# A tile's first matmul of the feed-forward stage in two pieces of 512 columns instead of eight of 128

## The chip, the cores and the metric

One core of a Trainium2 chip runs the whole kernel. The metric is the device time of one launch in microseconds (us); lower is better. The times before are the median, the lowest and the highest of 3 runs.

## What is computed

Four sets of 12608 tokens (128 features each) go through a set attention with 32 learned points, and then through a feed-forward block whose activation is a softmax times its own input, followed by a normalization.

```python
def mab(q, kv):
    s = scale * (q @ kv.transpose(0, 2, 1))
    s = s - s.max(-1, keepdims=True)
    a = np.exp(s)
    a /= a.sum(-1, keepdims=True) + 1e-09
    return a @ kv
h = mab(I, x)          # the 32 points look at a set's 12608 tokens
x = mab(x, h)          # each token looks at the set's 32 points
...
h = x @ w_in           # 128 -> 1024
e = np.exp(h - max(h))
solu = h * (e / sum(e))
ln = (solu - mean) / sqrt(var + 1e-06) * g_ln
out = ln @ w_out       # 1024 -> 128
```

Since the second attention only mixes 32 rows, the kernel multiplies these rows with `w_in` once for each set (`hs`, 32 x 1024, kept four times, once for each group of 32 partitions). A token's `x @ w_in` is then its 32 attention weights times `hs`: a matmul that contracts over 32 rows alone.

## The kernel before

**Tiles.** Tokens are worked in tiles of 128, 396 tiles in all (99 in each of 4 sets), four tiles to a group. For one tile, in this order: the first matmul (TensorE, line 1233) gives 128 x 1024 in PSUM (`h`, four such buffers of two banks each); VectorE (line 1275) multiplies by the softmax's divisor and takes the minimum; ScalarE (1286) takes the exponential and its sum; GpSimd (1290) multiplies the two; ScalarE (1301) squares for the variance; VectorE (1317) transposes in blocks of 32 x 32. When a group's four tiles are there, TensorE makes the second matmul (line 1473, called the products here) with `w_out`, again contracting over 32 rows at a time, 32 steps of four matmuls.

**Row groups.** TensorE's array is used as four strips of 32 rows (row groups 0 to 3), taken as two pairs: 0 and 1, 2 and 3. A tile's first matmul uses one pair, by the parity of the tile's place: row group `r` makes columns 0 to 511 in the first bank of `h`, `r + 1` columns 512 to 1023 in the second. Both of its pieces are 32 x 128 weights (`aT`, the tile's attention weights) against `hs`. The products of one half of a group use the same pair throughout, and two such streams (one for each pair) are under way most of the time.

**Order.** A planner written into the kernel fixes each engine's order of instructions before the launch. On TensorE it works in beats. A beat of products is one step of one or both streams (two or four matmuls of 129 columns). The function `beats` lays the first matmul's pieces between product steps of the other pair, called its companions here:

```python
for i in range(count):
    if also:
        also(i)
    went = 0
    for w in pairs:
        p = going(w, plan.now + i * BEAT)
        if p:
            p["emit"](2 * w, p["j"])
            p["emit"](2 * w + 1, p["j"])
            p["j"] += 1
```

Here `count` is 4, `pairs` is the other pair alone, and `also` is the function that the change touches. What the planner takes a beat to cost does not depend on `also`'s pieces. In the program, 350 of the 396 first matmuls have companions in all four beats, 21 in one to three, and 25 have none.

An f32 matmul appears in the trace as two instructions (called passes here), each with a weight load of its own in front (the weight load has its own row, PEld). So a first matmul is 16 passes before, eight on each of its two row groups.

Of the kernel before, what the change touches and what calls it, by code (L numbers as in the profile page):

```python
# [19 lines left out]
P = 128  # L20
# [121 lines left out]
class Planner:  # L142
# [8 lines left out]
    def spawn(self, gen, prio):  # L151
        self._step([gen, prio, 0], None)
# [8 lines left out]
    def give(self, lock, buf, *after):  # L161
        lock.free.append((buf, after))
        while lock.free and lock.waiting:
            lock.waiting.sort(key=lambda w: (w[2], w[1]))
            task = lock.waiting.pop(0)[0]
            self.blocked -= 1
            self._step(task, lock.free.pop(0))
# [96 lines left out]
def set_attention_then_solu_kernel(ctx: ExitStack, tc: tile.TileContext, x, inducing, w_in, w_out, g_ln, out):  # L264
# [30 lines left out]
    def buf(shape, name, dtype=F32, where=None):  # L295
        return (where or const).tile(shape, dtype, name=name)
# [66 lines left out]
    quarter = buf([P, 4], "quarter")  # L363
# [772 lines left out]
    def going(w, at):  # L1136

        for p in stream[w]:
            if p["j"] < JB:
                return p if p["ready"] <= at + EAGER else None  # L1140
        return None

    def load(w):
        return going(w, plan.now) is not None

    def beats(count, pairs=(0, 1), also=None):

        flow["took"] = 0
# [10 lines that stand above are left out]
                    went += 1  # L1159
            if not (went or also):  # L1160
                return i
            full = went + bool(also) > 1
            flow["took"] += BEAT + (TURN_ON if full and flow["half"] else 0)
            flow["half"] = not full
        return count

    def closing(d):

        for w in range(2):
            while stream[w] and stream[w][0]["j"] == JB:  # L1170
                flow["left"] -= 1
                stream[w].pop(0)["close"](d)
# [25 lines left out]
    def main():  # L1198
        t = 0
        for b in range(NB):  # L1200
            for j in order[b]:
                left = list(range(ff_groups[j][1]))
                spawn(open_group(b, j), t)
                while left:
                    for item in starts.get(t, ()):
                        spawn(*item)
                    near = left[:WINDOW_TILES]
                    rel = []
                    for s in near:
                        d = yield aT_ready[(b, ff_groups[j][0] + s)]  # L1210
                        rel += d
                    d = yield hw_ready[b]
                    rel += d
                    _, turn = yield TURN
                    hp, hrel = yield H.at(t + H_LAST)
                    op = Op("PE", 4 * BEAT, None, rel, hrel, prio=t - 50)
                    chosen = []

                    def mm1():
                        def slot(s):  # L1220
                            return part_of[b, ff_groups[j][0] + s][1]

                        s = min(near, key=lambda s: (load(slot(s) % 2), s))
                        chosen.append(s)
                        ka, i = part_of[b, ff_groups[j][0] + s]
                        aT, hs = aT_of[(b, ka)]["aT"][0], hT[b][1]
                        r = i % 2 * 2

                        def quarter(c):
                            for k in range(2):  # L1230
                                rows = slice((r + k) * M, (r + k + 1) * M)
                                cols = slice(k * 512 + c * P, k * 512 + (c + 1) * P)
                                nc.tensor.matmul(hp[:, cols], lhsT=aT[rows, i // 2, :], rhs=hs[rows, cols], start=True, stop=True)  # L1233

                        beats(4, (1 - i % 2,), quarter)
                        op.cost = flow["took"]

                    op.fn = mm1
                    d = yield op
                    closing(d)  # L1240
                    s = chosen[0]
                    left.remove(s)
                    if not left and j == order[b][-1]:
                        give(HW, hT[b], d)
                    spawn(soft(t, b, j, s, hp, d), t)
                    t += 1

    def open_group(b, j):
        G = grp[(b, j)]
        vt, rel = yield VT  # L1250
        plan.set(G["vt"], *rel)
        G["vtb"] = vt
        if fin_of[b, j][1] == 0:
            spawn(open_finish(b, fin_of[b, j][0]), 0)
        st, rel = yield ST
        G.update(st)
        G["stb"] = st
        plan.set(G["st"], *rel)
# [421 lines left out]
```

## Time and profile before

| | |
|---|---|
| time, median of 3 runs (lowest to highest) | 1202.43 us (1199.68 to 1202.57) |
| time of the profiled execution | 1208.28 us |
| its span, first to last instruction | 1206.5 us |
| mean granted TensorE clock | 0.987 of full speed |
| busy: TensorE, weight loads, VectorE, ScalarE, GpSimd | 97%, 90%, 90%, 92%, 88% |

Busy shares are of the span. A matmul's duration in the trace holds the time to run through the array, so that one instruction's duration is longer than the step to the next on the same row group, and several row groups at work count as one busy engine: 97% is not four full row groups.

### The profile page before, as it was taken

What the parts mean: (1) busy time and instruction counts of PE and PEld (TensorE: products, weight loads), DVE (VectorE), ACT (ScalarE), POOL (GpSimd) and SP (SyncE); (2) the same over time, 40 slices, a digit from 0 to 9 for tenths busy, and PEclk for the clock granted to TensorE, in tenths of its full rate; (3) what the DMA queues carried; (4) which work ended last, traced back from release to release, by engine and by line L of the source; (5) the groups of instructions that cost most, each with busy time, mean ns of one, the idle gap of its engine ahead of it and who ended that gap; (6) DMA issues with size and microseconds to landing.
All of it is one profiled execution on the core that took longest, in us unless ns stands there. A gap on an engine that the chain in (4) does not pass through costs nothing.

```text
span 1206.5 us, 77701 instructions
## 1 busy us (share of the span) xinstructions
PE 1166.9 (97%) x35388; PEld 1087.0 (90%) x35388; DVE 1079.9 (90%) x1639; ACT 1105.3 (92%) x2191; POOL 1063.6 (88%) x612
## 2 busy tenths in 40 slices
PE   8999999999999999999999999999999999999997
PEld 6789989999899899999898989899989999999996
DVE  6779889899899899989899898989999999899991
ACT  4689898999999999989998999999999999999995
POOL 2288789899899989898898998989999999999995
PEclk9959999999999999999999999999999999999999
DMA  9531433332132433332413343233312122220203
GB/s 342 211 125 53 131 83 101 108 105 56 49 97 69 141 110 117 102 89 61 117 40 101 92 139 118 86 106 89 99 40 81 42 46 57 75 64 6 48 6 86
DMA packets 166922, 111.24 MB, mean 92 GB/s; under 512 B 78112, under 2 KB 131776, under 8 KB 166464
## 3 DMA queue, kind: packets, MB, share of 16 engines
q1 hardware_dynamic: 166592, 106.27, 30.4%
q8 instruction: 277, 4.54, 1.6%
q14 instruction: 53, 0.43, 0.1%
HBM read 53.51 MB, written 52.17 MB: 88 GB/s over the span
## 4 chain that ended last, share of the span: by engine, by line
PE 47%; POOL 13%; ACT 10%; issue 4%; DVE 3%; DMA 1%; SPq 0%; ACTq 0%; POOLq 0%; DVEq 0%
PE h L1473 33%; POOL eu L1290 10%; PE h L1233 9%; ACT sq L1301 4%; ACT eu L1286 3%; POOL spare L1290 2%; PE h L655 1%; POOL spare L1547 1%; ACT spare L1501 1%; DVE hn L1275 1%; DVE vt L1317 1%; PE h L733 1%; PE h L850 1%; DVE spare L1275 1%; PE h L991 1%
## 5 line engine op out<-in xcount | busy, mean ns | idle before, releaser
L1473 PE MATMUL h<-wc,vt 32*128 32x129 f32 (+1 forms) x25344 | 996.2, 273 | 18.6 <-issue 10.7
L1473 PEld LDWEIGHTS h<-wc,vt 32*128 32x128 f32 (+1 forms) x25344 | 962.7, 185 | 46.2 <-issue 26.3
L1290 POOL TENSOR_TENSOR eu<-hn,eu 128x1024 f32<-128x1024 f32 x198 | 467.0, 2379 | 44.8 <-ACT eu L1286 43.7
L1233 PE MATMUL h<-hs,aT 32*128 32x128 f32 x6336 | 437.4, 277 | 5.7 <-issue 2.3
L1233 PEld LDWEIGHTS h<-hs,aT 32*128 32x128 f32 x6336 | 392.7, 189 | 22.5 <-issue 5.8
L1317 DVE STREAM_TRANSPOSE vt<-eu 128x1024 f32<-128x1024 f32 x327 | 397.2, 1228 | 8.6 <-POOL eu L1290 8.1
L1301 ACT ACTIVATE sq<-eu 128x1024 bf16<-128x1024 f32 x330 | 346.4, 1050 | 10.6 <-POOL eu L1290 5.5
L1290 POOL TENSOR_TENSOR eu<-spare,eu 128x1024 f32<-128x1024 f32 x132 | 311.8, 2378 | 14.7 <-ACT eu L1286 14.7
L1275 DVE TENSOR_SCALAR_CACHE_REDUCE hn<-h,rn 128x1024 f32<-128x1024 f32 x198 | 249.4, 1263 | 31.8 <-PE h L1233 23.2
L1275 DVE TENSOR_SCALAR_CACHE_REDUCE spare<-h,rn 128x1024 f32<-128x1024 f32 x198 | 248.9, 1263 | 30.2 <-PE h L1233 15.5
L1286 ACT ACTIVATE eu<-hn,nm 128x1024 f32<-128x1024 f32 x198 | 225.4, 1139 | 3.4 <-DVE hn L1275 3.1
L1290 POOL TENSOR_TENSOR spare<-spare 128x1024 f32<-128x1024 f32 x66 | 156.9, 2378 | 13.8 <-ACT spare L1286 13.8
L1286 ACT ACTIVATE eu<-spare,nm 128x1024 f32<-128x1024 f32 x132 | 150.4, 1140 | 2.4 <-DVE vt L1317 1.3
L1317 DVE STREAM_TRANSPOSE vt<-spare 128x1024 f32<-128x1024 f32 x65 | 80.0, 1231 | 1.5 <-POOL spare L1290 1.5
L1547 POOL TENSOR_TENSOR spare<-spare,fin 128x512 f32<-128x512 f32 x79 | 79.8, 1042 | 1.6
L1301 ACT ACTIVATE sq<-spare 128x1024 bf16<-128x1024 f32 x66 | 69.3, 1050 | 7.0 <-POOL spare L1290 5.4
L1286 ACT ACTIVATE spare<-spare,nm 128x1024 f32<-128x1024 f32 x66 | 75.2, 1140 | 0.5 <-DVE spare L1275 0.5
L1301 ACT ACTIVATION_READ_ACCUMULATOR sq<-eu 128x1 f32 x330 | 62.6, 190 | 0.0
L1501 ACT COPY spare<-h 128x774 f32<-128x774 f32 (+3 forms) x66 | 42.6, 648 | 13.6 <-PE h L1473 11.0
L655 PE MATMUL h<-ident,xn 32*128 32x32 f32 x1188 | 54.0, 227 | 0.7 <-issue 0.7
L655 PEld LDWEIGHTS h<-ident,xn 32*128 32x128 f32 x1188 | 51.1, 141 | 1.0 <-issue 1.0
L666 ACT COPY xT<-h 128x1024 f32<-128x1024 f32 (+2 forms) x42 | 38.0, 905 | 10.4 <-PE h L655 9.3
(189 smaller groups left out, 849.4 us busy)
## 6 DMA issues: line engine op xcount, KB each, us to landing
out_dram<-spare SPq DMA_DIRECT2D x95, 256.0 KB, 3.6
xT<-xd SPq DMA_DIRECT2D x93, 256.0 KB, 3.8
xn<-in_x_dram SPq DMA_DIRECT2D x73, 256.0 KB, 4.0
xd<-xT SPq DMA_DIRECT2D x72, 256.0 KB, 2.7
dl<-dd SPq DMA_DIRECT2D x392, 1.0 KB, 2.8
xd<-vt SPq DMA_DIRECT2D x7, 768.0 KB, 10.1
spare<-in_x_dram SPq DMA_DIRECT2D x5, 768.0 KB, 11.0
dd<-qe SPq DMA_DIRECT2D x95, 4.0 KB, 2.0
```

What stands on the lines that cost most here:

```text
L655: nc.tensor.transpose(out=tr[:, k * 512 + s * M : k * 512 + (s + 1) * M], in_=xn[r, s, :], identity=ident[r, r])
L666: lambda: nc.scalar.copy(xT.rearrange("c s (q t) -> c q s t", q=4)[:, 2 * w : 2 * w + 2, :n, :], tr.rearrange("c (k x) -> c k x", k=2)[:, ...
L733: nc.tensor.matmul(sc[g * M : (g + 1) * M, : nn * M], lhsT=indT, rhs=xT[:, :nn, g * M : (g + 1) * M], start=True, stop=True)
L1233: nc.tensor.matmul(hp[:, cols], lhsT=aT[rows, i // 2, :], rhs=hs[rows, cols], start=True, stop=True)
L1275: lambda: nc.vector.tensor_scalar(out=hn, in0=hp, scalar1=rn, scalar2=None, op0=ALU.mult, op1=ALU.min, accum_out=nm),
L1286: "ACT", 1133, lambda: nc.scalar.activation(e, hn, AF.Exp, bias=nm, scale=-1.0, accum_out=G["qe"][:, s, 1:2]), d, rel, srel,
L1290: d = yield Op("POOL", 2330, lambda: nc.gpsimd.tensor_tensor(out=e, in0=hn, in1=e, op=ALU.mult), de, prio=t + PR_MU)
L1301: "ACT", 1040, lambda: nc.scalar.activation(sq, e, AF.Square, scale=1.0 / 32.0, accum_out=G["qe"][:, s, 0:1]), d,
L1317: lambda: nc.vector.transpose(out=G["vtb"][:, : n * FF].rearrange("p (j s t) -> p j s t", j=M, s=n)[:, :, s, :], in_=e.rearrange("p (a f) ...
L1473: nc.tensor.matmul(op[:rows, a - 2 * w, :], lhsT=vt[q, k, :], rhs=wc[q, k, :], start=(k == 0), stop=(k == JB - 1))
L1501: return lambda: eng(to, at)
L1547: return lambda: eng.tensor_tensor(out=raw, in0=raw, in1=y[:, i0 : i0 + 4].unsqueeze(2).to_broadcast([rows, 4, C]), op=ALU.mult)
```

## The change

Each of the two row groups makes its 512 columns in one matmul. Both are issued in the first beat, ahead of the first companion; the companions of the other three beats follow with nothing in between.

```diff
-                        def quarter(c):
-                            for k in range(2):
+                        def whole(c):
+                            for k in range(2 if c == 0 else 0):
                                 rows = slice((r + k) * M, (r + k + 1) * M)
-                                cols = slice(k * 512 + c * P, k * 512 + (c + 1) * P)
+                                cols = slice(k * 512, (k + 1) * 512)
                                 nc.tensor.matmul(hp[:, cols], lhsT=aT[rows, i // 2, :], rhs=hs[rows, cols], start=True, stop=True)
 
-                        beats(4, (1 - i % 2,), quarter)
+                        beats(4, (1 - i % 2,), whole)
```

The order of the instructions changes on TensorE alone; on the other engines and in the DMA queues it is the same. On TensorE at a first matmul with companions, early in the first set, rows with - stand in the program before, with + in the changed one (`h_732` is the tile's buffer, `h_733` and `h_731` those of the two product streams, x2 means two matmuls):

```order
 L1473 MATMUL h_731<-wc,vt 128x129 x2
-L1233 MATMUL h_732<-hs,aT_94 128x128 x2
-L1473 MATMUL h_733<-wc,vt 128x129 x2
-L1233 MATMUL h_732<-hs,aT_94 128x128 x2
-L1473 MATMUL h_733<-wc,vt 128x129 x2
-L1233 MATMUL h_732<-hs,aT_94 128x128 x2
-L1473 MATMUL h_733<-wc,vt 128x129 x2
-L1233 MATMUL h_732<-hs,aT_94 128x128 x2
-L1473 MATMUL h_733<-wc,vt 128x129 x4
+L1233 MATMUL h_732<-hs,aT_94 128x512 x2
+L1473 MATMUL h_733<-wc,vt 128x129 x10
 L1473 MATMUL h_731<-wc,vt 128x129 x2
```

The four companion steps (eight matmuls; the last two of the ten belong to the next beat) now stand behind the whole first matmul. On TensorE at the start of the feed-forward stage there are no products yet, and first matmuls follow one another:

```order
 L991 MATMUL h_730<-vt,h_0_117 32x256 x4
-L1233 MATMUL h_732<-hs,aT_94 128x128 x8
-L1233 MATMUL h_733<-hs,aT_94 128x128 x8
-L1233 MATMUL h_730<-hs,aT_94 128x128 x8
+L1233 MATMUL h_732<-hs,aT_94 128x512 x2
+L1233 MATMUL h_733<-hs,aT_94 128x512 x2
+L1233 MATMUL h_730<-hs,aT_94 128x512 x2
```

There, eight matmuls become two at the same place.

## Rows read from the trace of the kernel before

**Rows 1.** The page's head: span, busy time of each engine.

```profile
span 1206.5 us, 77701 instructions
PE 1166.9 (97%) x35388; PEld 1087.0 (90%) x35388; DVE 1079.9 (90%) x1639; ACT 1105.3 (92%) x2191; POOL 1063.6 (88%) x612
```

**Rows 2.** Busy time by stretch; the first line names the columns.

```profile
core 0: us, PE busy (x) PEld busy (x) DVE busy (x) ACT busy (x) POOL busy (x), PEclk, DMA share, GB/s
...
120.00:1030.00 910.00, 889.37 (x28286) 833.40 (x28282) 840.58 (x1244) 861.66 (x1696) 834.64 (x474) 1.00 0.32 89
1030.00:1175.00 145.00, 142.58 (x4698) 139.52 (x4696) 137.26 (x181) 140.07 (x275) 144.84 (x79) 1.00 0.17 39
```

**Rows 3.** The page's chain that ended last: shares of the span.

```profile
PE 47%; POOL 13%; ACT 10%; issue 4%; DVE 3%; DMA 1%; SPq 0%; ACTq 0%; POOLq 0%; DVEq 0%
PE h L1473 33%; POOL eu L1290 10%; PE h L1233 9%; ACT sq L1301 4%; ACT eu L1286 3%; POOL spare L1290 2%; PE h L655 1%; POOL spare L1547 1%; ACT spare L1501 1%; DVE hn L1275 1%; DVE vt L1317 1%; PE h L733 1%; PE h L850 1%; DVE spare L1275 1%; PE h L991 1%
```

**Rows 4.** Groups of instructions, forms apart: count, busy us, mean ns, idle before.

```profile
L1473 PE MATMUL h<-wc,vt 32*128 32x129 f32 x24320 | 959.1, 274 | 17.6 <-issue 10.7 <-ACT spare L1501 2.8 <-DVE spare L1501 1.2
L1233 PE MATMUL h<-hs,aT 32*128 32x128 f32 x6336 | 437.4, 277 | 5.7 <-issue 2.3 <-DVE spare L1275 1.4 <-ACT aT L1072 0.7
...
L1233 PEld LDWEIGHTS h<-hs,aT 32*128 32x128 f32 x6336 | 392.7, 189 | 22.5 <-issue 5.8 <-DVE hn L1275 4.1 <-DVE spare L1275 2.8
```

**Rows 5.** TensorE in order of time, a first matmul with companions: start, length.

```profile
602.84 0.38 PE L1233 MATMUL h<-hs,aT 32*128 32x128 f32 x2
602.93 0.39 PE L1473 MATMUL h<-wc,vt 32*128 32x129 f32 x4
603.05 0.28 PE L1233 MATMUL h<-hs,aT 32*128 32x128 f32 x2
603.15 0.27 PE L1473 MATMUL h<-wc,vt 32*128 32x129 f32 x2
...
603.71 0.28 PE L1473 MATMUL h<-wc,vt 32*128 32x129 f32 x2
603.73 0.28 PE L1233 MATMUL h<-hs,aT 32*128 32x128 f32 x2
```

**Rows 6.** TensorE, matmuls of 512 columns one after another (line 933).

```profile
588.04 1.02 PE L933 MATMUL h<-w_in_sb,h 128*128 128x512 f32 x2
588.47 1.02 PE L933 MATMUL h<-w_in_sb,h 128*128 128x512 f32 x2
```

**Rows 7.** The chain between 488 and 500 us: start, share of chain.

```profile
490.39 0.10 PE h L1233
490.51 0.10 PE h L1233
...
491.07 0.11 PE h L1233 x2
```

**Rows 8.** The longest waits on TensorE's first matmul: us, times, longest.

```profile
DVE hn L1275 <- PE h L1233: 23.2, 28, 2.8
DVE spare L1275 <- PE h L1233: 15.5, 25, 1.4
```

**Rows 9.** TensorE, line 544, four matmuls of 512 columns on four row groups.

```profile
45.93 0.71 PE L544 MATMUL bank_e<-hn,fold 32*128 32x512 f32 x4
45.93 1.14 PE L544 MATMUL bank_e<-hn,fold 32*128 32x512 f32 x8
L544 PE MATMUL bank_e<-hn,fold x8: 587/640/692, 45.9 to 46.5; 32*128 32x512 f32 x8
```

**Rows 10.** VectorE at the first tiles: start, length, idle time before.

```profile
55.50 1.28 DVE L1275 TENSOR_SCALAR_CACHE_REDUCE hn<-h,rn 128x1024 f32<-128x1024 f32 x1 [0.17 <-PE h L1233]
56.71 0.08 DVE L1275 DVE_READ_ACCUMULATOR hn<-h,rn 128x1 f32 x1
56.71 1.28 DVE L1275 TENSOR_SCALAR_CACHE_REDUCE hn<-h,rn 128x1024 f32<-128x1024 f32 x1
```

## The prediction

> **What bounds the kernel now.** I read the head of the page first, then the busy time by stretch, then the chain that ended last, then the single instructions. The head [rows 1] shows no engine that stands out: all five rows lie between 88% and 97%. The stretches [rows 2] say more. From 120 to 1030 us, three quarters of the span, ScalarE is busy for 861.66 of 910 us (95%), GpSimd for 834.64 (92%), VectorE for 840.58 (92%). From 1030 to 1175 us GpSimd is busy for 144.84 of 145 us: there nothing that TensorE does can help, as long as it isn't late. TensorE's own 889.37 of 910 can't be read as a share of its capacity, because two row groups at work look as busy as four. So I go to the chain [rows 3]: 47% of the span runs through TensorE, 33% through the products of line 1473 and 9% through the first matmul of line 1233; GpSimd has 13%, ScalarE 10%. TensorE's order sets the end for about half of the time, in the long middle stretch, and three other engines are a few per cent behind it. That is what limits any gain on TensorE: it is paid on the chain's share, and soon the next engine is the latest.
>
> What a first matmul costs on its two row groups is read from two places. With companions [rows 5] its passes start at 602.84, then 603.05, and from there to 603.73 in six steps: 0.68 / 6 = 0.113 us for 128 columns (the first step is 0.21 us long, since the first weight load has nothing to hide behind). On the chain [rows 7] it is the same: 490.39 to 491.07 in six steps. The companions keep the same step beside it (602.93, 603.15, ..., 603.71). So eight passes take 8 x 0.113 = 0.90 us.
>
> **What the change removes.** Of 6336 passes with as many weight loads [rows 4] a quarter stays, 1584 of each. The trace has no first matmul of 512 columns, but the nearest row shows what a pass of that length takes on a row group when its weights are there in time: on line 933 the starts are 588.04 and 588.47, a step of 0.43 us [rows 6]. That is 128 rows deep, not 32; the one place with 32 rows and 512 columns [rows 9] agrees: four matmuls on four row groups, eight passes, in 1.14 us, where the first passes last 0.692 and the second 0.587. The second four end at 47.07, so their starts are 47.07 - 0.59 = 46.48, 0.55 after the first; 0.692 - 0.587 = 0.105 of it is the weight load in front, which leaves 0.44, with up to 0.02 of the four's own spread in it. So two passes take 0.86 us in place of 0.90: **0.04 us less on the pair for each tile**. The 392.7 us of weight loads of line 1233 [rows 4] mostly disappear as busy time, but they are worth no more than this: they lay beside the passes, and that a pass of 128 columns steps at 0.113 where a quarter of 0.43 would be 0.108 is all that they can have cost.
>
> **What it adds.** Nothing. No instruction, wait or DMA is added, and the order on the other four engines is the same.
>
> **What it moves.** With companions (350 of 396 first matmuls in all four beats) the second to fourth companion stood behind a piece of the first matmul; now all stand behind the whole of it. Whether they start as early depends on whether TensorE lets an instruction for idle row groups pass one that waits for its own. Each first matmul puts two passes on each row group: the second must wait 0.43 us for the first, and everything behind it in the program belongs to the other pair. Line 544 [rows 9] decides this as far as a row here can. In the program its four matmuls follow one another, each with its two passes; in the first 0.1 us four passes have started, all at 45.93, and all eight are over after 1.14 us. Were the second matmul held until the first one's second pass had started, the four would need five steps of 0.43 us, 2.15 us and the run through the array. So TensorE does let later row groups pass. What that place doesn't show is a stream of short passes, sixteen of them, running past a long one that waits. Bounds for the companions: from below, nothing (they keep their step of 0.113); from above, they are held for one pass, 0.43 us. I take nothing, since the row is much nearer to it.
>
> The Trainium skill has a rule that speaks against this: "TensorE: Matmul & The Clock Gate", Part 3, "The mechanism", says that matmuls start and end strictly in program order with no reordering, and that weight loads alone are pulled ahead. By that rule every companion would wait for the second long pass, and line 544 would take over 2 us. The trace shows 1.14 us there, so I follow the row and keep the rule as a rival.
>
> Without companions (25 cases) the next instruction reached its row groups late before, because fourteen more passes stood ahead of it in the queue after the first two, and now two do. That could be worth up to about 0.9 - 0.43 = 0.47 us each, 12 us in all. I take nothing: most of these stand at the start of the feed-forward stage, and there VectorE works through the tiles back to back (55.50, 56.71; 1.28 us each [rows 10]), so that a first matmul that is ready earlier waits for VectorE instead.
>
> VectorE waits for the first matmul 28 + 25 times, 38.7 us in all [rows 8]. Each of these waits gets shorter by at least 0.04 us, 2 us together; that is the same saving seen from the other engine, and isn't added.
>
> **The sum.** All 396 tiles, if each were on the chain: 396 x 0.04 = 16 us. On the chain are 9% of 1206.5 = 109 us of line 1233 [rows 3], which is 109 / 0.90 = 120 tiles: 120 x 0.04 = 4.8 us. Part of it will be taken up by ScalarE and GpSimd, which are only 5% and 8% from full in the middle stretch [rows 2]; I round down to 4.4 us. The profiled execution took 1208.28 us around its span of 1206.5; the sum takes it to 1203.9. The runs without a profile have a median of 1202.43, 5.85 us less, and I carry the saving over unchanged: 1202.43 - 4.4 = **1198.0 us**, 0.37% faster. A difference under 0.3% (3.6 us) can hardly be told from none, as the three runs of before already lie 2.9 us apart.
>
> **The rivals.**
>
> *The saving is hidden.* The chain passes from engine to engine in thousands of short pieces, and the path behind it may be late by less than 0.04 us at most places. For it: three engines between 92% and 95% in the middle stretch, and GpSimd at 100% after 1030 us [rows 2]. Against it: long pieces of the chain stay on TensorE, as the run of steps at 490 us [rows 7]. The time would be 1202.43 less 0 to 2: about 1201.5 us.
>
> *The companions wait.* By the rule of order, or because row groups 2 and 3 can't take new weights while those for a second pass lie loaded and wait, the other pair stands still for up to 0.43 us at each of 350 first matmuls: 150 us if all were on the chain, with the chain's share of the tiles (120 of 396) 45 us, less 4.8: about 1243 us. A hold of one short step, 0.113 us, would cost 350 x 0.113 x 0.30 = 12, less 4.8: about 1210 us. It decides from a mean hold of 0.05 us per first matmul, where 350 x 0.05 x 0.30 = 5.2 us eats the saving. Against it: line 544 [rows 9]. For it: no row here shows short passes running past a long one.
>
> *A larger gain.* The first matmul no longer advances in step with its companions: if these are late, it no longer waits for them. If the two pairs were often out of step, more than the chain's 120 tiles would gain, up to the 16 us above: 1186 us. Against it: in rows 5 both pairs keep the same 0.113, neither waits for the other.
>
> **How the numbers follow.** The forecast (3.6 to 9 us faster) gets 0.43, the larger gain 0.05, the hidden saving 0.40, the waiting companions 0.12. So faster 0.48, the same 0.40, slower 0.12. The range: 1190 below (half of the chance of the larger gain lies beneath), 1206 above, the edge of no change at 1202.43 + 3.6; of the 0.12 beyond it, a hold just above 0.05 us still falls near it. That leaves out about 0.15. The forecast's own range is 1193 to 1199.
>
> **What will show it.** Right: line 1233 has 1584 passes, 0.43 us apart on a row group; the companions' first pass starts within 0.1 us of the first matmul's and the next follow in steps of 0.11 while the long passes run; VectorE's waits for line 1233 are no longer than before; the chain's share of line 1233 falls a little. The prediction fails if the companions show gaps of 0.3 to 0.4 us beside a long pass (slower), if passes of 512 columns on 32 rows step by 0.45 us or more (no saving), or if the chain moves to ScalarE or GpSimd at the places where TensorE got shorter (hidden).

## The result, and the profile after

The changed kernel takes 1186.26 us (median of 6 runs, 1182.92 to 1189.1) against 1202.5 us for the kernel before in the same comparison (6 runs, 1195.92 to 1211.9): a ratio of 0.9844, with a 95% interval of 0.9814 to 0.9874. The ratio is taken within each set of three runs, so that it is not exactly the quotient of these medians. The kernel is 1.6% faster, 16 us by the medians and 19 us by the ratio, about four times what was forecast, and outside the range.

The page of the profile after answers to [rows 1, 3]; q8 is the queue that brings TensorE's instructions:

```profile
span 1181.1 us, 68196 instructions
...
PE 1151.1 (97%) x30636; PEld 1055.0 (89%) x30636; DVE 1074.8 (91%) x1639; ACT 1102.6 (93%) x2191; POOL 1065.6 (90%) x612
...
q8 instruction: 239, 3.92, 1.4%
...
PE 45%; POOL 23%; ACT 20%; issue 7%; DVE 3%; DMA 2%; SPq 0%; ACTq 0%; POOLq 0%; DVEq 0%
PE h L1473 32%; POOL eu L1290 16%; ACT sq L1301 9%; ACT eu L1286 6%; PE h L1233 4%; POOL spare L1290 3%; POOL spare L1547 3%; ACT spare L1286 1%; ACT xT L666 1%; ACT spare L1501 1%; PE h L850 1%; PE h L655 1%; ACT a L1013 1%; PE bank_e L557 1%; DMA dl<-dd 1%
```

4752 passes and as many weight loads are gone (35388 to 30636). The chain's share of the first matmul fell from 9% to 4%; GpSimd and ScalarE rose from 23% to 43% together: they are the latest more often, while TensorE's own share is nearly the same in these two profiles (47% and 45%). By stretch, to be held against [rows 2]:

```profile
54.00:120.00 66.00, 62.03 (x1354) 47.84 (x1354) 65.18 (x99) 63.76 (x114) 58.58 (x28) 0.95 0.33 99
120.00:1030.00 910.00, 899.05 (x25033) 835.49 (x25028) 854.28 (x1265) 879.50 (x1732) 854.44 (x483) 1.00 0.32 90
1030.00:1150.00 120.00, 116.92 (x3292) 111.99 (x3288) 113.44 (x148) 114.24 (x231) 119.84 (x67) 0.99 0.14 30
```

In the same 910 us every other engine does more work (GpSimd 854 us in place of 835). The last stretch stays GpSimd's alone (119.84 of 120) and is only shorter because less is left for it. The granted clock from 54 to 120 us is 0.95 in this execution; in the profile of before it is:

```profile
54.00:120.00 66.00, 63.42 (x1434) 55.96 (x1430) 59.15 (x90) 57.24 (x102) 52.41 (x25) 0.79 0.28 85
```

By the trace's clock records TensorE was at the lower of its two levels (1.2 GHz) from 62.4 to 89.7 us in the profile of before, and from 68.6 to 75.4 us in this one; in the 54 us ahead of this stretch it had made 556 and 566 passes. This differs by execution in both kernels: two more profiles of the kernel before (below) have 0.87 and 0.77 in this stretch, a second one of the changed kernel 0.87. So some of the 25.4 us between the two spans (1206.5 and 1181.1) belongs to these two executions, and the sizes below are taken from ratios.

The first matmul itself, in the groups that answer to [rows 4], and one of them in order of time, as [rows 5]:

```profile
L1473 PE MATMUL h<-wc,vt 32*128 32x129 f32 x24320 | 946.6, 273 | 9.1 <-ACT spare L1501 2.3 <-DVE spare L1501 2.1 <-DVE spare L1275 1.5
L1233 PE MATMUL h<-hs,aT 32*128 32x512 f32 x1584 | 419.6, 607 | 6.0 <-DVE spare L1275 2.6 <-ACT spare L1501 1.0 <-DVE hn L1275 0.9
```

```profile
597.00 0.70 PE L1233 MATMUL h<-hs,aT 32*128 32x512 f32 x2
597.02 0.72 PE L1473 MATMUL h<-wc,vt 32*128 32x129 f32 x8
597.54 0.59 PE L1233 MATMUL h<-hs,aT 32*128 32x512 f32 x2
```

Eight companion passes start from 597.02 on, beside the first long passes and before the second at 597.54 (0.54 later, 0.11 of it the first weight load): they run past the waiting pass. It is so in general: in the middle stretch the largest step between two product starts beside a first matmul has a median of 0.11 us in both kernels, by the traces' records. So the rule of strict order is not what this chip did here either ("TensorE: Matmul & The Clock Gate" of the Trainium skill, Part 3, "The mechanism").

What the prediction had not looked at is idle time of TensorE that no releaser explains, "issue" in the waits. Before:

```profile
PE h L1473 <- issue: 10.7, 19, 1.3
...
PE h L1233 <- issue: 2.3, 5, 0.8
...
PE h L655 <- issue: 0.7, 2, 0.4
```

After, with VectorE's waits for the first matmul beside it (22.2 us in 32 waits, from 38.7 in 53 [rows 8]):

```profile
DVE hn L1275 <- PE h L1233: 12.2, 18, 1.5
...
DVE spare L1275 <- PE h L1233: 10.0, 14, 1.3
...
PE h L1473 <- issue: 0.5, 2, 0.3
...
PE h L1057 <- issue: 0.2, 1, 0.2
```

13.7 us became 0.7. The longest of these stops in the profile before, in order of time:

```profile
527.48 0.27 PE L1473 MATMUL h<-wc,vt 32*128 32x129 f32 x1
529.02 0.38 PE L1473 MATMUL h<-wc,vt 32*128 32x129 f32 x2 [1.27 <-issue]
```

and the DMA engines in 40 slices of the stretch from 521 to 530 us, with the packets of q8 in it, then the packets from 527.58 to 529.02:

```profile
DMA  9998898998978992499899988200000000000000
...
q8 instruction: 2, 0.03, 1.3%
```

```profile
DMA packets 0, 0.00 MB, mean 0 GB/s; under 512 B 0, under 2 KB 0, under 8 KB 0
```

The DMA engines are busy for most of the time until about 527. Of the two q8 packets the second lies in that tail: it begins at 526.59 and ends at 527.58. TensorE runs dry at 527.75, nothing else is moving, and it goes on at 529.02, 1.44 us after the packet's end. This is no single case. Each of the 25 stops over 0.15 us between 100 and 1000 us in that trace ends 1.25 to 1.62 us after the end of a q8 packet, and all stand at the same place in a count by 256 of TensorE's instructions (the place drifts from 177 to about 115 between the first and the last of them, as the few instructions that aren't matmuls or loads aren't in the count). In the second and third profile of the kernel before (below) 13 and 17 such stops stand at the same places, 1.25 to 1.57 us behind a packet. Four of the 25, worked out from the trace's records:

```
stop us   ends at   last q8 packet from, to    end to end   place in 256
0.71      137.16    134.74   135.66            1.50         177
1.16      141.99    139.14   140.55            1.43         176
0.57      236.05    233.67   234.63            1.43         170
1.27      529.02    526.59   527.58            1.44         149
```

277 packets carry 2 x 35388 instructions, 256 each, in 4.54 MB, 16 KB each. The Trainium skill says the same of these blocks ("Runtime: NRT & Kernel Launch", "Instruction fetch mechanics": blocks of 16 KiB, 256 instructions); it also says that their cost is mostly hidden, and there the traces differ: in the middle stretch half of all runs of 256 of TensorE's instructions take 4.0 us or less (after the change 4.5), and by the same records about a third of the blocks begin less than 1.6 us after their packet has ended, as those behind a stop do.

### The profile page after: what moved, and what is told of

It reads as the page before. It is cut to its first block, busy times and chain, and to the rows that moved or that the text cites. A ratio compares the mean times of both kernels' runs of the same rounds, so it can differ in the third digit from the quotient of the medians.

```text
span 1181.1 us, 68196 instructions
## 1 busy us (share of the span) xinstructions
PE 1151.1 (97%) x30636; PEld 1055.0 (89%) x30636; DVE 1074.8 (91%) x1639; ACT 1102.6 (93%) x2191; POOL 1065.6 (90%) x612
## 4 chain that ended last, share of the span: by engine, by line
PE 45%; POOL 23%; ACT 20%; issue 7%; DVE 3%; DMA 2%; SPq 0%; ACTq 0%; POOLq 0%; DVEq 0%
PE h L1473 32%; POOL eu L1290 16%; ACT sq L1301 9%; ACT eu L1286 6%; PE h L1233 4%; POOL spare L1290 3%; POOL spare L1547 3%; ACT spare L1286 1%; ACT xT L666 1%; ACT spare L1501 1%; PE h L850 1%; PE h L655 1%; ACT a L1013 1%; PE bank_e L557 1%; DMA dl<-dd 1%
## 5 line engine op out<-in xcount | busy, mean ns | idle before, releaser
L1473 PE MATMUL h<-wc,vt 32*128 32x129 f32 (+1 forms) x25344 | 983.5, 273 | 10.4 <-ACT spare L1501 3.1
L1233 PE MATMUL h<-hs,aT 32*128 32x512 f32 x1584 | 419.6, 607 | 6.0 <-DVE spare L1275 2.6
L1317 DVE STREAM_TRANSPOSE vt<-eu 128x1024 f32<-128x1024 f32 x327 | 397.7, 1229 | 11.4 <-POOL eu L1290 10.7
L1290 POOL TENSOR_TENSOR eu<-spare,eu 128x1024 f32<-128x1024 f32 x132 | 311.7, 2379 | 11.2 <-ACT eu L1286 11.1
L1233 PEld LDWEIGHTS h<-hs,aT 32*128 32x128 f32 x1584 | 124.6, 186 | 27.5 <-DVE spare L1275 8.1
```

Of the source, the lines that this page charges most:

```text
L1290: d = yield Op("POOL", 2330, lambda: nc.gpsimd.tensor_tensor(out=e, in0=hn, in1=e, op=ALU.mult), de, prio=t + PR_MU)
L1317: lambda: nc.vector.transpose(out=G["vtb"][:, : n * FF].rearrange("p (j s t) -> p j s t", j=M, s=n)[:, :, s, :], in_=e.rearrange("p (a f) ...
L1473: nc.tensor.matmul(op[:rows, a - 2 * w, :], lhsT=vt[q, k, :], rhs=wc[q, k, :], start=(k == 0), stop=(k == JB - 1))
```

## The experiments

Two theories stood at the start. **Supply**: fewer instructions are needed from memory, so TensorE runs dry less often. **Pass length**: the prediction's own, 0.86 us for 0.90. A third, **order**: the gain comes from issuing the first matmul at once. All times are against the kernel before on the same chip; medians and intervals are those of five rounds where an interval is given.

**Eight pieces at once.** Pieces of 128 columns as before, in the order of the change:

```diff
-                            for k in range(2 if c == 0 else 0):
...
-                                cols = slice(k * 512, (k + 1) * 512)
...
+                            at = 0
+                            for size in (128, 128, 128, 128) if c == 0 else ():
+                                for k in range(2):
...
+                                    cols = slice(k * 512 + at, k * 512 + at + size)
...
+                                at += size
```

> The first matmul in eight pieces of 128 columns as in the kernel before, but all eight issued in the first beat, ahead of the companions, as in the changed kernel. It has the order of the change and the instruction count and pass length of before. Theory of instruction supply (the time went where TensorE ran out of instructions: 13.7 us of idle time with no releaser in the profile before, 0.7 after; fewer instructions, fewer such stops): about as slow as before (ratio 0.99 to 1.01), TensorE's idle time put down to issue at 8 to 18 us. Theory of order (the companions and the next instruction pass earlier because the whole first matmul is issued at once): as fast as the changed kernel, ratio 0.985, issue time not decisive. Theory of pass length (0.86 for 0.90 us): as slow as before.

Measured: 1335.14 us, ratio 1.114 (1.111 to 1.117). No theory said this. In order of time, a first matmul (its line is 1235 here, the products' 1476):

```profile
600.97 0.72 PE L1235 MATMUL h<-hs,aT 32*128 32x128 f32 x10
601.43 0.38 PE L1476 MATMUL h<-wc,vt 32*128 32x129 f32 x2
601.52 0.38 PE L1235 MATMUL h<-hs,aT 32*128 32x128 f32 x3
```

Ten passes, five for each row group, start before the companions may, 0.46 us after the first (also the median of the middle stretch). So there is a hold, but it comes from passes that queue up for a busy row group, not from one that waits: two passes ahead let the companions by, eight don't. 136 us / 396 = 0.34 us a tile. With this hold TensorE has 94% of the chain, and the waits show no idle time of it without a releaser, where supply expected 8 to 18 us. Order alone is no gain.

**Two halves at once**, and **400 + 112 columns at once**: as above with these sizes.

> The first matmul in two pieces of 256 columns on each row group, all in the first beat: 16 instructions a tile with the weight loads, against 32 before and 8 after. A pass of 256 columns is long enough to hide its weight load, so the pair is busy for about 0.86 us, as in the changed kernel. Pass length: the whole gain, ratio 0.985. Instruction supply: two thirds of the instructions that the change saves are saved, so two thirds of the gain or more, ratio 0.985 to 0.990, and issue idle of TensorE 1 to 6 us, between 13.7 and 0.7. Order: the whole gain.

> The first matmul in pieces of 400 and 112 columns, all in the first beat: as many instructions as the run in halves, but the piece of 112 columns steps at 0.112 like a weight load, so that the pair is busy for 2 x 0.336 + 2 x 0.112 = 0.90 us, as long as before. Pass length: no gain, ratio 1.00. Instruction supply: the same as the run in halves, within 0.3%. Order: the whole gain.

Measured: 1197.85 us, ratio 0.9997 (0.9973 to 1.0021), and 1198.70 us, 1.0002 (0.9981 to 1.0022). Idle with no releaser is 1.3 and 1.8 us, as supply said, but the time didn't follow. TensorE has 69% and 79% of the chain (47%, 66% and 52% in the three profiles of the kernel before), and by the traces' records the largest step between two product starts beside a first matmul has a median of 0.21 us in the middle stretch, in place of 0.11. So four passes ahead of the companions bring part of the hold that eight bring; these two runs mix it with what they were to measure, and were made anew, spread over the beats (below).

**More instructions without work.** In every beat:

```diff
         for i in range(count):
+            for _ in range(2):
+                nc.tensor.keepalive_nop([nc.tensor.lower_ap(ident[:1, :1])])
             if also:
```

> The changed kernel with two instructions in each beat that only count a semaphore up on TensorE's sequencer: 8822 more instructions, nearly the 9504 that the change removed; matmuls, weight loads and their order as in the changed kernel. Instruction supply: back to the time of before, ratio 0.99 to 1.01, issue idle of TensorE 8 to 18 us again. Pass length and order: as fast as the changed kernel, ratio 0.985, unless the sequencer's own time for them, some 0.05 us each, holds matmuls back; that would show as a slowdown without longer issue stops.

Measured: 1682.03 us, ratio 1.402. That is (1682 - 1182) / 8822 = 0.057 us for each added instruction, with 1182 us for the changed kernel by its ratio. In the trace each lasts 0.051 us on TensorE's sequencer, 450 us together: hardly anything of it is hidden. Idle time with no releaser rose to 55.8 us, most of it on the products (line 1475 here):

```profile
PE h L1475 <- issue: 47.0, 89, 1.7
```

Supply had expected 8 to 18 us. As the sequencer's own time sets the pace here, the run doesn't decide between the theories. Such an instruction is no free filler on TensorE.

**Two halves, spread**, and **400 + 112, spread**: the second piece in the third beat (halves, shown) or in the fourth (`{0: [(0, 400)], 3: [(400, 112)]}`), companions between:

```diff
-                            for k in range(2 if c == 0 else 0):
...
-                                cols = slice(k * 512, (k + 1) * 512)
...
+                            for at, size in {0: [(0, 256)], 2: [(256, 256)]}.get(c, ()):
+                                for k in range(2):
...
+                                    cols = slice(k * 512 + at, k * 512 + at + size)
...
```

> As the run in halves, but the second half is issued in the third beat, with two companion steps between the halves, so that no more than four passes of the first matmul stand ahead of a companion in the queue of the program. In the run with both halves at once the idle time with no releaser was down to 1.3 us, and the time was still that of before; in the run with eight pieces at once the companions were held and the time was 11% longer. Theory of instruction supply with a hold behind passes issued at once: the hold is gone here, the supply is as good as in the run in halves, so a ratio of 0.987 to 0.993. Theory of pass length: the same as the run in halves at once, 1.00, since that run had the short passes and gained nothing. Theory that only the whole matmul issued at once brings the gain: 1.00.

> Pieces of 400 columns in the first beat and of 112 in the fourth: the pair is busy as long as before (0.90 us), companions stand between the pieces as before, and the instruction count is half of before's for this matmul. Instruction supply: a ratio of 0.987 to 0.995, idle time with no releaser on TensorE under 3 us. Pass length: 1.00.

> The changed kernel once more, as the measure for the other runs of this chip. Every theory: ratio 0.982 to 0.988.

Measured: halves 1184.97 us, ratio 0.9860 (0.9836 to 0.9885); 400 + 112 1189.67 us, 0.9898 (0.9875 to 0.9921); the changed kernel again 1184.29 us, 0.9854 (0.9830 to 0.9878). The waits of the 400 + 112 run, where the products' line is 1474, and of the changed kernel's second profile:

```profile
PE h L1474 <- issue: 3.1, 8, 0.7
...
PE h L655 <- issue: 0.4, 1, 0.4
```

```profile
PE h L1473 <- issue: 0.8, 1, 0.8
...
PE h L1057 <- issue: 0.4, 1, 0.4
```

These are the runs that tell. With the pair nearly as busy as before (0.89 us in the trace, 0.90 before) and companions between the pieces, half the passes of the first matmul give 1201.22 x (1 - 0.9898) = 12.3 us. The shorter time of the pair at the same count (halves, 0.87 us, against 400 + 112) gives another 1201.22 x 0.0038 = 4.6 us, though these two intervals overlap, and the second piece also stands in another beat. Issuing the matmul whole adds nothing to that that can be measured.

The granted clock has a part in these sizes. In this comparison the executions of the kernel before have mean granted clocks of 0.984 to 0.990, those of the changed kernel 0.988 to 0.995. Over the executions whose clock is on record, 59 of the kernel before and 11 of the changed one, the time is 0.63 and 0.64 us longer for each 0.001 less. By an estimate that holds the clock equal, the changed kernel is 13 us faster than the kernel before, halves 13 and 400 + 112 10, each within 2 us. The shorter time of the pair is then worth about 2.5 us. Whether the change itself shortens the time at the lower level isn't shown.

**The first matmul in a later beat**, the fourth (shown) and the second:

```diff
-                            for k in range(2 if c == 0 else 0):
+                            for k in range(2 if c == 3 else 0):
```

> The changed kernel with the two matmuls of 512 columns issued in the fourth beat, behind three companion steps. Instruction count and passes are those of the changed kernel; the first matmul ends later against its companions by up to three beats, 0.67 us, and stands beside the next instructions instead. Instruction supply and pass length: idle time with no releaser stays at 0 to 2 us, and the ratio within 0.6% of the changed kernel's, 0.98 to 0.99. Theory of order (the gain comes from the first matmul being issued whole and early): most of the gain is lost, ratio 0.995 to 1.01.

> The changed kernel with the two matmuls of 512 columns issued in the second beat, behind one companion step, with three companion steps behind them. In the fourth beat the ratio was 1.044 in place of 0.985. If companions are needed behind a long pass, since the next beats' products for the same pair fill its queue and hold those of the other pair: three steps are left, a hold of about one step, 0.22 us, at part of the tiles, ratio 0.99 to 1.01. If the place does not matter by itself and the fourth beat was slow for the late end of the first matmul alone: a third of the loss, 1.00 to 1.01. If only the very last beat is bad: 0.985.

Measured: in the fourth beat 1252.87 us, ratio 1.044 (1.041 to 1.047), in the second 1182.12 us, 0.9861 (0.9835 to 0.9887), no worse than in the first. The fourth beat, in order of time:

```profile
604.88 0.70 PE L1233 MATMUL h<-hs,aT 32*128 32x512 f32 x2
604.98 0.61 PE L1473 MATMUL h<-wc,vt 32*128 32x129 f32 x8
605.41 0.59 PE L1233 MATMUL h<-hs,aT 32*128 32x512 f32 x2
605.43 0.81 PE L1473 MATMUL h<-wc,vt 32*128 32x129 f32 x12
```

The other pair's passes keep their step of 0.11 us beside the first long pass and on from 605.43, until 605.66 in the trace's records; then none starts before 605.84, when the second long pass, begun at 605.41, has had its 0.43 us. In the middle stretch the largest step between any two pass starts at this place has a median of 0.18 us, and of 0.11 in the changed kernel. Behind the first matmul now stand beats of both pairs, and the products for the busy pair queue up in front of the other pair's. The rival of the waiting companions thus had a counterpart in a real hold; what decides, by this reading, is what stands behind the long pass. That is read from the order and the gap and not tried by itself; the second beat, with three companion steps behind, agrees. Supply and pass length, which both said 0.98 to 0.99, missed it too.

**Less data traffic.** A quarter of the output is stored; the rest of it stays unwritten:

```diff
-            d = yield dma(n * P * C * 4, lambda: nc.sync.dma_start(to, os), done, trel, issue=1150)
+            d = yield dma(n * P * C * 4, lambda: nc.sync.dma_start(to[:, :1, :], os[:, :1, :]), done, trel, issue=1150)
```

> The kernel before with a quarter of the output stored (one token of four; the rest of the output is left unwritten), so that 19 MB of 106 MB of data transfers fall away. The instructions of TensorE, VectorE, ScalarE and GpSimd are the same, one by one. Instruction supply, with blocks of instructions that come late because they share the DMA engines with data: TensorE's idle time with no releaser falls from 13.7 us to 7 to 12 us, and the time by about as much as the idle time, ratio 0.990 to 0.998. Theory that an instruction costs time in itself (in issue or weight loading), wherever it comes from: ratio 0.998 to 1.002 and the idle time as before.

> The changed kernel with a quarter of the output stored, as the control of the run above. Its idle time with no releaser is about 1 us already, so by the theory of instruction supply less traffic gives it less than it gives the kernel before: within 0.3% of the changed kernel's ratio of 0.985. If it gains as much as the kernel before does, the traffic matters in another way than through instructions.

Measured: before 1194.39 us, ratio 0.9974 (0.9958 to 0.9991), idle with no releaser 4.7 us; changed 1183.17 us, 0.9876 (0.9851 to 0.9901), 0.9 us. The waits of the two runs:

```profile
PE h L1473 <- issue: 4.7, 8, 1.1
```

```profile
PE h L1473 <- issue: 0.9, 1, 0.9
```

The instructions are the same, and the kernel before gets a little faster with fewer bytes beside them, while the changed kernel does not. That is what supply says, but the idle time fell by 9 us against the first profile and the time by 3.1.

**The spread of the kernel before.**

> The kernel before, for a second profile of it. If its idle time with no releaser is typical at 13.7 us, this gives 11 to 16 us; if the first profile caught a bad execution, 5 to 10 us.

> The kernel before, for a third profile of it: as the second, 5 to 16 us of idle time with no releaser.

Measured: one execution each, 1196.81 and 1200.84 us. The second profile, and then the third:

```profile
PE h L1473 <- issue: 6.3, 12, 0.9
...
PE h L1233 <- issue: 1.9, 3, 1.0
```

```profile
PE h L1473 <- issue: 6.4, 13, 1.0
...
PE h L1233 <- issue: 1.9, 4, 0.8
```

8.2 and 8.3 us, not 13.7: the first profile belongs to a longer execution, 1208.28 us. Against these, less traffic took 3.6 us of idle time away and 3.1 us of time.

**More instructions in another place.** The attentions' score matmuls of the changed kernel in pieces of 64 columns (line 733 shown, 991 alike):

```diff
-            for g in range(4):
...
+            step = n if early else 2
+            for c0 in range(0, n, step):
+                for g in range(4):
+                    nn = n if (not half or (g + 1) * M <= half) else nf
+                    c1 = min(c0 + step, nn)
+                    if c1 > c0:
...
+                            sc[g * M : (g + 1) * M, c0 * M : c1 * M], lhsT=indT, rhs=xT[:, c0:c1, g * M : (g + 1) * M], start=True, stop=True
```

> The changed kernel with the two attentions' score matmuls (lines 733 and 991) cut into pieces of 64 columns after the start stage: 1174 more matmuls, 4696 more instructions, half of what the change removed; the first matmul, the products and the order are those of the changed kernel, and a piece of 64 columns is longer than its weight load of 32 columns, so that the array is not busy longer. Instruction supply: idle time with no releaser rises from about 1 us to 3 to 8 us, the time by 3 to 7 us, ratio to before 0.988 to 0.993. Theory of the queue on the first matmul's row groups: unchanged, 0.983 to 0.987, idle time about 1 us.

Measured: 1190.18 us, ratio 0.9924 (0.9899 to 0.9949). The page's instructions and the waits (line 854 is the attention's sum, 1483 the products):

```profile
PE 1160.2 (97%) x32984; PEld 1089.8 (92%) x32984; DVE 1077.1 (90%) x1639; ACT 1103.9 (93%) x2191; POOL 1064.1 (89%) x612
```

```profile
PE h L854 <- issue: 2.0, 4, 1.1
PE h L1483 <- issue: 1.5, 3, 1.0
```

The first matmul and its queue are untouched, and 4696 more instructions cost 0.9924 - 0.9854 = 0.0070, 8.4 us (4 to 13 with both intervals). Some of that is array time: a cut score stage takes 1.10 us from its first start to its last end in the trace where a whole one takes 1.07, over 48 stages about 1.5 us. The rest, some 7 us, comes with the instructions; idle time with no releaser rose from 1.2 (in the changed kernel's second profile) to 3.5 us.

## Why the prediction was wrong

- **What bounds.** Right: the middle stretch was TensorE's and the last one GpSimd's, and all of the gain lies ahead of that last stretch.
- **Pass length.** Right in mechanism: in the trace the two long passes start 0.43 us apart, as forecast. What this is worth is not measured well enough to call the 4.8 us on the chain (4.4 after rounding down) right: 4.6 us between halves and 400 + 112 has overlapping intervals, is about 2.5 at equal clock, and the beat of the second piece differs too.
- **Nothing is added, the companions pass.** Right for this order, by the rows at 597 us. The rival had its place and its price (1.11 and 1.044 in two runs), but needs more passes ahead of the companions, or none of them behind.
- **The step that failed** is in "What the change removes": the 4752 passes and weight loads that go away "are worth no more than" the 0.04 us of pass time. As instructions they were worth two thirds of the gain or more: 12.3 us (10 at equal clock) with nearly the pass time of before and only 6336 of the 9504 instructions gone. One row showed the place: [rows 4], with 10.7 us of idle time on the products that ended on "issue". The 4% of the chain on "issue" in [rows 3] is no such mark, as it is 7% after the change. I read the releasers that had a name and left the one that had none.
- **The larger gain** came near the number (1186) by luck: its mechanism was a first matmul freed from its companions' step, but in halves, spread, it still goes in pieces between them, and the gain is the same within the intervals.
- **The hidden saving.** It did not come about: the time fell by more than the pass time that was saved.
- **Without companions.** Not tried alone.

So the main cause is shown: fewer instructions, 10 to 12 us with 6336 of the 9504 gone. The shorter passes add a few us, which no run separates well. That blocks of instructions come late, and less often with fewer of them, is shown by the places of the stops and by the runs with more instructions elsewhere and with less traffic.

Idle time with no releaser fell from 8.2 to 1.2 us between executions of 1196.81 and 1184.54 us, 7 us. That counts too little of each stop, since a pass of the products lasts 0.27 us in the trace, while passes start every 0.04 us on average: much of a stop is hidden behind the last pass. So I counted gaps of over 0.2 us from one pass's start to the next, with no releaser, less 0.04 us each, by how long they end after a q8 packet (from 60 us on to 20 us before the end, us in all):

| profile | 0.7 to 1.2 us after | 1.2 to 1.7 us after | 1.7 to 2.2 us after |
|---|---|---|---|
| before, second and third | 4.9 and 5.2 | 19.3 and 19.3 | 3.9 and 4.3 |
| before, less traffic | 4.2 | 12.9 | 4.7 |
| 400 + 112, spread | 10.1 | 15.8 | 6.4 |
| changed, first and second | 6.6 and 4.4 | 7.4 and 5.9 | 8.7 and 8.6 |
| changed, more instructions elsewhere | 3.7 | 11.1 | 3.6 |

The kernel before has 15 us there beyond its neighbours, the changed kernel none; 12 to 15 us of stops are gone, enough for the gain that the passes leave. With more instructions elsewhere some 7 us come back, as much as the time. In the 400 + 112 run 7 of the 10 to 12 us are found in this way; the others stay open, and the first matmul's shorter queue may have a part in them, which no run here separates.

## What to carry to other kernels

Count an engine's instructions as a cost of their own when it finishes them about as fast as they come from memory: here half of all runs of 256 of TensorE's took 4.0 us or less. Idle time "by issue" with no releaser, just behind a packet of the instruction queue and at a nearly fixed place in a count by 256, was its mark here, and longer matmuls the cure, even where they saved little array time. When matmuls on separate row groups are to overlap, keep few passes of one group ahead of the other's in the program (eight at once cost 11%), and put the other's work behind a long pass (without it, 4.4%).

## What was not expected of the hardware

- A stop for instructions ends 1.25 to 1.62 us after the block's packet has ended, with no other DMA packet moving (527.58 to 529.02).
- TensorE let four short passes on each of two idle row groups run past a waiting long one (597.02 to 597.54). With eight short passes queued on each busy row group it held the other pair until five of the eight had started (0.46 us).
- An instruction without work lasts 0.051 us on TensorE's sequencer and cost 0.057 us of time (the run of 1682.03 us), where passes start every 0.04 us on average (1181.1 / 30636).
